# Four float32r products whose moving operand is read as two halves in turn

## The chip, the cores and the metric

The kernel runs on one core of a Trainium2 chip. The metric is the device time of one execution in microseconds (us). PE is TensorE's matmul side, PEld its weight loads, DVE is VectorE, ACT ScalarE, POOL GpSimd, SP the engine that issues most DMAs. In a product (matmul) the stationary operand is loaded into the array first; the moving operand is then streamed through it column by column, and the result goes to PSUM.

## The reference

```
X = fft(fft(x, axis=1), axis=2).real           # x: 8 x 3072 x 256
h = X @ w_in;  g = h - tanh(h);  y = g @ w_out # 256 -> 2048 -> 256, tokens: 8 * 3072
h = y @ w_in2                                  # 256 -> 1024
e = exp(h - max(h));  s = e / (sum(e) + 1e-9)
v = h * s                                      # then a layer norm over 1024, times g_ln
out = layernorm(v) * g_ln @ w_out2             # 1024 -> 256
```

All arrays are float32.

## The kernel before

The first stage (up to about 200 us) computes the transform along the sequence with cosine and sine tables in plain float32 (`products`, L445) and a few float32r corrections (`lone_products`, L457). The transform along the model dimension is folded into `w_in` (`fold_w_in`, L345). What is left of the transform goes to DRAM and comes back in 48 groups of 256 pairs of tokens (`load_z`), six groups for each of the 8 batches.

After that the kernel makes 768 steps: 48 groups `n` times 16 blocks `m` of 128 of the 2048 hidden features. A step holds, in the order in which each engine's instructions are issued:

- `ab` (L720): six float32r products with a moving operand of 256 columns of `zs`, into a tile `pab`. They make an even and an odd part.
- `act_out` of the step before: `g = h - t` on DVE (L754), then the split of `g` into `gh`: ACT rounds it to float32r (`rnd`, L152), and POOL makes the remainder (`rest`, L155).
- `act_in`: `asb`, and the sum and difference `h` on DVE (L727, L742, L743), then tanh on ACT (L749).
- `o1` of two steps before: six products (L773) with 512 columns of `gh` moving, summed over the 16 steps of a group in `x2p`.

The second layer is spread over the steps, one tile of 128 tokens in each four of them: `h2` (L806, twelve products with 512 columns of `wi2` moving, in two steps of six), `expo` and `soft` on DVE and ACT, a transpose by DVE and DMA, `split_moved` on ACT and POOL, and `outp` (L896, 24 products with 256 columns of `wo2` moving, in two steps of twelve). The order is written out by hand in the loop over the steps; no planner moves anything. Each engine works through its own queue in order.

Every float32r product is made as three passes: high part times high part, high times low, low times high. So each moving operand exists twice, as a rounded high part and a remainder, made by `rnd` and `rest`. `split_z` does so for `zs` in steps 9 and 11 of the group before it is used; `split_wi2` and `split_wo2` do it once for each half of the weights, in steps 10, 12, 18 and 19. The queue of SP carries the loads and stores; the change moves none of them.

The host puts the output's rows in order by a table (`out_rows`).

Of the kernel before, what the change touches and what calls it, by code (L numbers as in the profile page):

```python
# [19 lines left out]
B, S, D = 8, 3072, 256  # L20
FF1, FF2 = 2048, 1024
P = 128
# [5 lines left out]
GP = 256  # L28
GPB = PAIRS // GP
# [36 lines left out]
def columns():  # L66

    i = np.arange(NS)
    odd = 2 * i.reshape(NSJ, P) + 1
    return np.concatenate([np.stack([odd, S // 2 - odd], 1).reshape(-1), 4 * i + 2, 4 * i])  # L70
# [42 lines left out]
def out_rows():  # L113

    k = columns()
    plus = np.where(k % 4 == 3, k, (S - k) % S)
    minus = np.where(k % 4 == 3, S - k, k)
    minus[k == 0] = S // 2
    rows = np.stack([plus.reshape(GPB, GP), minus.reshape(GPB, GP)], 1).reshape(-1)
    return (np.arange(B)[:, None] * S + rows[None]).reshape(-1)  # L120


# [5 lines left out]
def fft2_moe_moe_kernel(  # L128
    ctx: ExitStack, tc: tile.TileContext, xr, x8, xn, xn8, w_in, w_out, w_in2, w_out2, g_ln, tt, t8, ft, out
):  # L130
    nc = tc.nc
# [19 lines left out]
    def rnd(o, i):  # L151
        nc.scalar.activation(out=o, in_=i, func=AF.Copy)  # L152

    def rest(eng, o, i, hi):
        eng.tensor_tensor(out=o, in0=i, in1=hi.bitcast(F32), op=ALU.subtract)  # L155

    def doubles(ap):

        return ap.bitcast(U32)
# [29 lines left out]
    wt = [wa.tile([P, 2, 2, 512], F32R, name=f"wt{c}") for c in range(4)]  # L189
# [35 lines left out]
    def split_z(n, u):  # L225
        zf, nb, zs = zg[n]
        if n % GPB >= NSJ:
            rnd(zs[:, 0, u], zf[:, u])
            rest(nc.gpsimd, zs[:, 1, u], zf[:, u], zs[:, 0, u])
        else:  # L230
            zc = zp.tile([P, GP], F32, tag="zc", bufs=1, name=f"zc{n}_{u}")
            for w, op in enumerate((ALU.add, ALU.subtract)):
                nc.gpsimd.tensor_tensor(out=zc[:, w * P : (w + 1) * P], in0=zf[:, u, :P], in1=zf[:, u, P:], op=op)
            rnd(zs[:, 0, u], zc)
            rest(nc.gpsimd, zs[:, 1, u], zc, zs[:, 0, u])


    coming, raws = [], {}
# [100 lines left out]
    def fold_w_in(c, w):  # L339

        pws = []
        for mt in range(2):
            pw = ps.tile([P, 512], F32, tag="ps", name=f"pw{c}_{mt}")
            for k in range(2):
                nc.tensor.matmul(  # L345
                    pw,
                    ftab[:, k, mt * P : (mt + 1) * P],
                    w[:, k * 512 : (k + 1) * 512],
                    start=(k == 0),
                    stop=(k == 1),  # L350
                )
            pws.append(pw)
        wf = fold.tile([P, 1024], F32, tag="cw", bufs=3, name=f"wf{c}").rearrange("p (m n) -> p m n", m=2)
        for mt, pw in enumerate(pws):
            rnd(wf[:, mt], pw)
        nc.gpsimd.dma_start(out=wnu_d[:, c * 512 : (c + 1) * 512], in_=wf[0:1, 1])
        rnd(wt[c][:, 0], wf)
        rest(nc.vector, wt[c][:, 1], wf, wt[c][:, 0])
        nc.gpsimd.memset(wt[c][0:1, :, 1].bitcast(F32), 0.0)
# [268 lines left out]
    def taken(banks, shape, tag, name):  # L628
        banks.append(banks.pop(0))
        return banks[-1].tile(shape, F32, tag=tag, name=name)  # L630


    wi2 = wp.tile([P, 2, 2, FF2], F32R, name="wi2")

    wi2_raw = [wk.tile([P, FF2], F32, tag="stage", name=f"wi2r_{k}") for k in range(2)]
# [1 line left out]
        nc.sync.dma_start(out=wi2_raw[k], in_=wi2_d[k])  # L637

    def split_wi2(k):
        rnd(wi2[:, 0, k], wi2_raw[k])  # L640
        rest(nc.gpsimd, wi2[:, 1, k], wi2_raw[k], wi2[:, 0, k])

    wo2 = wp.tile([P, 2, NK2, D], F32R, name="wo2")
    ident = wp.tile([P, P], F32, name="ident")
# [6 lines left out]
    wg = []  # L651
# [21 lines left out]
        )  # L673

    def split_wo2(half):
        g = wg[half][1]
        ks = slice(half * 4, half * 4 + 4)
        rnd(wo2[:, 0, ks], g)
        rest(nc.gpsimd, wo2[:, 1, ks], g, wo2[:, 0, ks])


    a1536 = wp.tile([P, NM, B], F32, name="a1536")
# [29 lines left out]
    x2p, x2s = {}, {}  # L712

    def ab(n, m):
        _, nb, zs = zg[n]
        c, o = m // 4, (m % 4) * P
        pab = p_ab.tile([P, 2, GP], F32, tag="ab", name=f"ab{n}_{m}")
        for u in range(2):
            for i, (hw, hz) in enumerate(PASSES):
                nc.tensor.matmul(  # L720
                    pab[:, u], wt[c][:, hw, u, o : o + P], zs[:, hz, u], start=(i == 0), stop=(i == 2)
                )
        return pab

# [40 lines left out]
    def o1(n, m):  # L765
        if m == 0:
            x2p[n] = [p_x2.tile([P, 2 * GP], F32, tag=f"x2_{mt}", name=f"x2p{n}_{mt}") for mt in range(2)]
        gh = gs.pop((n, m))
        c, k = divmod(m, 4)

        for i, (hw, hg) in enumerate(((0, 0), (1, 0), (0, 1))):
            for mt in range(2):
                nc.tensor.matmul(  # L773
                    x2p[n][mt],
                    wo1[c][:, hw, k, mt * P : (mt + 1) * P],
                    gh[:, hg],
                    start=(m == 0 and i == 0),
                    stop=(m == NM - 1 and i == 2),
                )
        if m == NM - 1:  # L780
            xs = wk.tile([P, 2, 2, 2 * GP], F32R, tag="x2s", name=f"x2s{n}")
            x2s[n] = xs
            if n == NG - 1:
                for mt, p in enumerate(x2p.pop(n)):
                    rnd(xs[:, 0, mt], p)
                    rest(nc.vector, xs[:, 1, mt], p, xs[:, 0, mt])
                return
            xf = wk.tile([P, 2, 2 * GP], F32, tag="stage", name=f"x2f{n}")
            for mt, p in enumerate(x2p.pop(n)):
                rnd(xf[:, mt], p)  # L790
            for mt in range(2):
                rnd(xs[:, 0, mt], xf[:, mt])
                rest(nc.gpsimd, xs[:, 1, mt], xf[:, mt], xs[:, 0, mt])
# [3 lines left out]
    def h2(n, i, f):  # L797
        xs = x2s[n]
        if f == 0:
            h2s[n, i] = taken(bank_h2, [P, FF2], "h2", f"ph2_{n}_{i}")  # L800
        ph = h2s[n, i]
        tk = slice(i * P, (i + 1) * P)
        fs = slice(f * 512, (f + 1) * 512)
        for k in range(2):
            for q, (hx, hw) in enumerate(PASSES):
                nc.tensor.matmul(  # L806
                    ph[:, fs],
                    xs[:, hx, k, tk],
                    wi2[:, hw, k, fs],
                    start=(k == 0 and q == 0),  # L810
                    stop=(k == 1 and q == 2),
                )
# [74 lines left out]
    def outp(n, i, half):  # L887
        if half == 0:
            pos[n, i] = taken(bank_o, [P, 512], "t", f"po{n}_{i}")
        po = pos[n, i]  # L890
        ut = uts.pop((n, i, half))
        for k4 in range(4):
            k = half * 4 + k4
            ks = slice(k4 * P, (k4 + 1) * P)
            for q, (hu, hw) in enumerate(PASSES):
                nc.tensor.matmul(  # L896
                    po[:, :D],
                    ut[:, hu, ks],
                    wo2[:, hw, k],
                    start=(k == 0 and q == 0),  # L900
                    stop=(k == NK2 - 1 and q == 2),
                )
        if half == 1:
            o = wk.tile([P, D], F32, tag="o", name=f"o{n}_{i}")
            nc.scalar.activation(out=o, in_=po[:, :D], func=AF.Copy, scale=sts.pop((n, i))[:, 10:11])  # L905
            r0 = (n * 4 + i) * P
            nc.sync.dma_start(out=out[r0 : r0 + P, :], in_=o)
            us.pop((n, i))
            pos.pop((n, i))
# [39 lines left out]
    for step in range(steps + 2):  # L949
        n, j = divmod(step, NM)  # L950
        if step < steps:
            pab = ab(n, j)
            asb = lead(n, j, pab) if n == 0 else None
# [9 lines left out]
        for s in (range(o1_done, min(s1 + 1, steps))):  # L963
            o1(*divmod(s, NM))
        o1_done = max(o1_done, min(s1 + 1, steps))
        layer2(step, False)
        if step in (4, 8):
            c = (4, 8).index(step) + 2
# [4 lines left out]
        if step in (10, 12):  # L973
            split_wi2((step - 10) // 2)
# [15 lines left out]
        if NM + 2 <= step < NM + 4:  # L990
            split_wo2(step - NM - 2)
        if j == 6 and 1 <= n and n + 1 < NG:
            load_z(n + 1)
        if 1 <= n and n + 1 < NG and j in (9, 11):
            split_z(n + 1, int(j > 9))
# [11 lines left out]
    for f in range(2):  # L1007
        outp(NG - 2, 1, f)
# [3 lines left out]
    for f in range(2):  # L1012
        outp(NG - 2, 2, f)
    for f in range(2):
        h2(*tiles[1], f)
# [64 lines left out]
```

## Time and profile before

| | |
|---|---|
| median of three timed runs | 2922.41 us (2921.7 to 2923.3) |
| the profiled execution: its span, from the first to the last instruction | 2923.9 us |
| granted TensorE clock over the span | 0.997 of full speed |
| instructions | 49792, of them 16799 products and as many weight loads |
| HBM read and written | 162.01 and 138.47 MB |

The page gives no other time of the profiled execution than its span, which lies 1.5 us above the median. A matmul's time in the trace runs from its start to its last result, so the times of products that follow each other overlap; what a product takes of the engine is seen in the distance from one start to the next. Busy time counts overlapping stretches once. An idle time belongs to the engine before which it stands, and behind `<-` is what ended it.

### The profile page before, as it was taken

The page shows a single profiled execution, that of the slowest core. Times are in us where ns is not written, and L with a number is a line of the kernel's source. Part 1 is how long each engine was busy: PE and PEld are TensorE (multiplying, and loading weights), DVE is VectorE, ACT ScalarE, POOL GpSimd, SP SyncE. Part 2 cuts the span into 40 slices and gives each one's busy share as a digit, 9 for nine tenths or more (in the row PEclk, how much of TensorE's full clock was granted, in tenths as well). Part 3 has the DMA queues.
Part 4 walks back from the last instruction along what each step waited for, and adds up shares of the span by engine and source line. Part 5 has one row for each costly group of instructions (what it writes and reads, how often), then busy time and mean ns, then how long its engine had stood idle before and what let it go on. Part 6 is the DMA issues. An engine that isn't in the chain of part 4 may idle for free. (4 is left out here: it accounts for less than half of the span.)

```text
span 2923.9 us, 49792 instructions
## 1 busy us (share of the span) xinstructions
PE 2881.3 (99%) x16799; PEld 2482.3 (85%) x16799; DVE 2403.0 (82%) x4818; ACT 1803.9 (62%) x3287; POOL 1965.2 (67%) x2413
## 2 busy tenths in 40 slices
PE   7899999999999999999999999999999999999999
PEld 3467888888888888888888888888888888888888
DVE  7897888888888888888888888888888888888885
ACT  2345666666666666666666666666666666666665
POOL 0156767777677776777777767777677766777763
PEclk9999999999999999999999999999999999999999
DMA  8781333343334334344334433443434443443331
GB/s 306 252 298 31 88 94 94 90 94 92 87 94 98 89 89 99 88 94 93 89 95 91 96 89 90 97 91 90 94 92 92 93 92 88 95 98 89 89 91 42
DMA packets 876512, 303.75 MB, mean 104 GB/s; under 512 B 788520, under 2 KB 837688, under 8 KB 872960
## 3 DMA queue, kind: packets, MB, share of 16 engines
q1 hardware_dynamic: 873536, 293.95, 40.9%
q10 hardware_dynamic: 2304, 6.29, 0.5%
q8 instruction: 132, 2.16, 0.3%
q14 instruction: 124, 1.02, 0.1%
q0 software_dynamic: 416, 0.33, 0.0%
HBM read 162.01 MB, written 138.47 MB: 103 GB/s over the span
## 5 line engine op out<-in xcount | busy, mean ns | idle before, releaser
L155 POOL TENSOR_TENSOR gh<-g,gh 128x512 fp32r<-128x512 f32 x768 | 993.2, 1297 | 469.3 <-ACT gh L152 469.3
L773 PE MATMUL x2p<-gh,wo 128*128 128x512 f32 x4608 | 1206.5, 397 | 3.6 <-POOL gh L155 2.3
L773 PEld LDWEIGHTS x2p<-gh,wo 128*128 128x128 f32 x4608 | 825.5, 189 | 166.3 <-POOL gh L155 10.7
L749 ACT ACTIVATE t<-h 128x512 f32<-128x512 f32 x768 | 459.5, 598 | 547.8 <-DVE h L743 446.3
L720 PEld LDWEIGHTS ab<-zs,wt 128*128 128x128 f32 x4608 | 649.0, 188 | 72.5 <-DVE h L743 2.7
L720 PE MATMUL ab<-zs,wt 128*128 128x256 f32 x4608 | 668.0, 280 | 2.1 <-DVE h L743 2.1
L754 DVE TENSOR_TENSOR g<-h,t 128x512 f32<-128x512 f32 x768 | 521.8, 679 | 172.0 <-ACT t L749 168.5
L152 ACT ACTIVATE gh<-g 128x512 fp32r<-128x512 f32 x768 | 480.9, 626 | 235.5 <-DVE g L754 223.1
L896 PE MATMUL po<-wo,ut 128*128 128x256 f32 x4608 | 597.8, 278 | 4.4 <-ACT ut L152 2.6
L806 PE MATMUL ph<-wi,x2s 128*128 128x512 f32 x2304 | 597.1, 394 | 0.0
L896 PEld LDWEIGHTS po<-wo,ut 128*128 128x128 f32 x4608 | 560.7, 188 | 10.1 <-POOL ut L155 5.0
L727 DVE SCALAR_TENSOR_TENSOR asb<-nb,wnu,ab 128x256 f32<-128x256 f32 x768 | 367.1, 478 | 221.1 <-PE ab L720 219.3
L806 PEld LDWEIGHTS ph<-wi,x2s 128*128 128x128 f32 x2304 | 420.0, 188 | 84.5
L155 POOL TENSOR_TENSOR ut<-um,ut 128x512 fp32r<-128x512 f32 x372 | 480.8, 1292 | 0.8 <-issue 0.8
L743 DVE TENSOR_TENSOR h<-asb,ab 128x256 f32<-128x256 f32 x768 | 328.8, 428 | 26.5
L742 DVE TENSOR_TENSOR h<-asb,ab 128x256 f32<-128x256 f32 x768 | 329.1, 429 | 26.2
L819 ACT ACTIVATE e<-ph,st 128x1024 f32<-128x1024 f32 x192 | 214.3, 1116 | 97.9 <-DVE st L817 82.1
L817 DVE TENSOR_REDUCE st<-ph 128x1 f32<-128x1024 f32 x192 | 233.6, 1216 | 3.5 <-PE ph L806 3.5
L825 DVE SCALAR_TENSOR_TENSOR u<-ph,e 128x1024 f32<-128x1024 f32 x192 | 233.6, 1217 | 0.0
L152 ACT ACTIVATE ut<-um 128x512 fp32r<-128x512 f32 x372 | 231.1, 621 | 0.0
L856 DVE STREAM_TRANSPOSE tb<-u 128x1024 f32<-128x1024 f32 x186 | 230.0, 1236 | 0.0
L836 ACT ACTIVATE e<-u,st 128x1024 f32<-128x1024 f32 x192 | 219.5, 1143 | 0.0
(101 smaller groups left out, 1531.2 us busy)
## 6 DMA issues: line engine op xcount, KB each, us to landing
mv_d<-tb SPq DMA_DIRECT2D x186, 512.0 KB, 2.6
um<-mv_d SPq DMA_DIRECT2D x744, 128.0 KB, 3.8
out<-o SPq DMA_DIRECT2D x192, 128.0 KB, 1.7
x<-xr SPq DMA_DIRECT2D x23, 1024.0 KB, 7.6
z_d<-zt SPq DMA_DIRECT2D x16, 384.0 KB, 7.4
z_d<-zt ACTq DMA_DIRECT2D x16, 384.0 KB, 6.6
wo<-w_out SPq DMA_DIRECT2D x24, 256.0 KB, 5.5
zf<-z_d SPq DMA_DIRECT2D x48, 128.0 KB, 3.3
```

Source lines behind the costliest of these rows:

```text
L152: nc.scalar.activation(out=o, in_=i, func=AF.Copy)
L155: eng.tensor_tensor(out=o, in0=i, in1=hi.bitcast(F32), op=ALU.subtract)
L720: nc.tensor.matmul(pab[:, u], wt[c][:, hw, u, o : o + P], zs[:, hz, u], start=(i == 0), stop=(i == 2))
L727: nc.vector.scalar_tensor_tensor(out=asb, in0=zg[n][1], scalar=wnu[:, m : m + 1], in1=pab[:, 0], op0=ALU.mult, op1=ALU.add)
L742: nc.vector.tensor_tensor(out=h[:, 0], in0=asb, in1=pab[:, 1], op=ALU.add)
L743: nc.vector.tensor_tensor(out=h[:, 1], in0=asb, in1=pab[:, 1], op=ALU.subtract)
L749: nc.scalar.activation(out=t, in_=h, func=AF.Tanh)
L754: nc.vector.tensor_tensor(out=g, in0=hs.pop((n, m)).rearrange("p u n -> p (u n)"), in1=ts_.pop((n, m)).rearrange("p u n -> p (u n)"), op=A ...
L773: nc.tensor.matmul(x2p[n][mt], wo1[c][:, hw, k, mt * P : (mt + 1) * P], gh[:, hg], start=(m == 0 and i == 0), stop=(m == NM - 1 and i == 2),)
L806: nc.tensor.matmul(ph[:, fs], xs[:, hx, k, tk], wi2[:, hw, k, fs], start=(k == 0 and q == 0), stop=(k == 1 and q == 2),)
L817: nc.vector.tensor_reduce(out=st[:, 0:1], in_=ph, axis=AX.X, op=ALU.max, negate=True)
L896: nc.tensor.matmul(po[:, :D], ut[:, hu, ks], wo2[:, hw, k], start=(k == 0 and q == 0), stop=(k == NK2 - 1 and q == 2),)
```

## The change

In four products (`ab`, `o1`, `h2`, `outp`) the moving operand's access pattern is changed: instead of columns 0, 1, 2, ... of a row of 512 or 256 columns, TensorE reads column 0 of the first half, column 0 of the second half, column 1 of the first, and so on (`in_turn`). The results go to neighbouring places of PSUM in the order in which they come (`in_pairs` only gives the output the same shape). So the result's columns stand in another order than the operand's.

For `zs`, `wi2` and `wo2` that is undone beforehand: the splits now put the even columns into the first half and the odd ones into the second, so that reading in turn restores the old order. For `gh` it is not undone: the tokens of a group then stand as sum, difference, sum, difference instead of all sums and then all differences, and the host's table `out_rows` is changed to match.

```diff
-    rows = np.stack([plus.reshape(GPB, GP), minus.reshape(GPB, GP)], 1).reshape(-1)
+    rows = np.stack([plus, minus], 1).reshape(-1)
...
+    def in_turn(ap):
+        return ap.rearrange("p (h n) -> p n h", h=2)
+
+    def in_pairs(ap):
+        return ap.rearrange("p (n h) -> p n h", h=2)
+
+    def split_halves(eng, hi, lo, whole):
+
+        by_half = whole.rearrange("p (n h) -> p h n", h=2)
+        hi, lo = (a.rearrange("p (h n) -> p h n", h=2) for a in (hi, lo))
+        rnd(hi, by_half)
+        rest(eng, lo, by_half, hi)
...
         if n % GPB >= NSJ:
-            rnd(zs[:, 0, u], zf[:, u])
-            rest(nc.gpsimd, zs[:, 1, u], zf[:, u], zs[:, 0, u])
+            split_halves(nc.gpsimd, zs[:, 0, u], zs[:, 1, u], zf[:, u])
...
     def split_wi2(k):
-        rnd(wi2[:, 0, k], wi2_raw[k])
-        rest(nc.gpsimd, wi2[:, 1, k], wi2_raw[k], wi2[:, 0, k])
+        raw = wi2_raw[k].rearrange("p (f n h) -> p f h n", f=2, h=2)
+        hi, lo = (wi2[:, q, k].rearrange("p (f h n) -> p f h n", f=2, h=2) for q in range(2))
+        rnd(hi, raw)
+        rest(nc.gpsimd, lo, raw, hi)
...
     def split_wo2(half):
-        g = wg[half][1]
+        g = wg[half][1].rearrange("p k (n h) -> p k h n", h=2)
         ks = slice(half * 4, half * 4 + 4)
-        rnd(wo2[:, 0, ks], g)
-        rest(nc.gpsimd, wo2[:, 1, ks], g, wo2[:, 0, ks])
+        hi, lo = (wo2[:, q, ks].rearrange("p k (h n) -> p k h n", h=2) for q in range(2))
+        rnd(hi, g)
+        rest(nc.gpsimd, lo, g, hi)
...
                 nc.tensor.matmul(
-                    pab[:, u], wt[c][:, hw, u, o : o + P], zs[:, hz, u], start=(i == 0), stop=(i == 2)
+                    in_pairs(pab[:, u]),
+                    wt[c][:, hw, u, o : o + P],
+                    in_turn(zs[:, hz, u]),
...
                 nc.tensor.matmul(
-                    x2p[n][mt],
+                    in_pairs(x2p[n][mt]),
                     wo1[c][:, hw, k, mt * P : (mt + 1) * P],
-                    gh[:, hg],
+                    in_turn(gh[:, hg]),
...
-                    ph[:, fs],
+                    in_pairs(ph[:, fs]),
                     xs[:, hx, k, tk],
-                    wi2[:, hw, k, fs],
+                    in_turn(wi2[:, hw, k, fs]),
...
-                    po[:, :D],
+                    in_pairs(po[:, :D]),
                     ut[:, hu, ks],
-                    wo2[:, hw, k],
+                    in_turn(wo2[:, hw, k]),
```

## Rows read from the trace of the kernel before

**Rows 1.** The page's busy line: busy us (share of the span) and count for each engine.

```profile
PE 2881.3 (99%) x16799; PEld 2482.3 (85%) x16799; DVE 2403.0 (82%) x4818; ACT 1803.9 (62%) x3287; POOL 1965.2 (67%) x2413
```

**Rows 2.** Windows, two stretches: us, busy us (count) by engine, granted clock, DMA share, GB/s.

```profile
700.00:1500.00 800.00, 799.90 (x4797) 705.49 (x4796) 665.30 (x1361) 515.79 (x941) 574.68 (x709) 1.00 0.40 93
2870.00:2924.00 54.00, 47.41 (x314) 42.02 (x312) 26.60 (x55) 26.99 (x51) 13.24 (x35) 1.00 0.07 22
```

**Rows 3.** The page's costliest groups: line, operation, tiles, shapes, count, busy us, mean ns, idle.

```profile
L773 PE MATMUL x2p<-gh,wo 128*128 128x512 f32 x4608 | 1206.5, 397 | 3.6 <-POOL gh L155 2.3
...
L720 PE MATMUL ab<-zs,wt 128*128 128x256 f32 x4608 | 668.0, 280 | 2.1 <-DVE h L743 2.1
...
L896 PE MATMUL po<-wo,ut 128*128 128x256 f32 x4608 | 597.8, 278 | 4.4 <-ACT ut L152 2.6
L806 PE MATMUL ph<-wi,x2s 128*128 128x512 f32 x2304 | 597.1, 394 | 0.0
```

**Rows 4.** Timeline of PE in two stretches: start us, us, engine, line, operation, count.

```profile
236.39 3.62 PE L666 MATMUL cm<-wg,ones 128*128 128x256 f32 x16
...
1500.28 0.87 PE L720 MATMUL ab<-zs,wt 128*128 128x256 f32 x6
1500.99 1.56 PE L773 MATMUL x2p<-gh,wo 128*128 128x512 f32 x6
1502.39 1.55 PE L806 MATMUL ph<-wi,x2s 128*128 128x512 f32 x6
1503.78 0.87 PE L720 MATMUL ab<-zs,wt 128*128 128x256 f32 x6
...
1507.98 1.54 PE L896 MATMUL po<-wo,ut 128*128 128x256 f32 x12
1509.36 1.56 PE L773 MATMUL x2p<-gh,wo 128*128 128x512 f32 x6
...
1514.26 0.87 PE L720 MATMUL ab<-zs,wt 128*128 128x256 f32 x6
```

**Rows 5.** Products by line: count, shortest/median/longest ns, first and last start, forms.

```profile
L457 PE MATMUL pz<-t8s,hl x48: 326/326/687, 30.8 to 191.2; 96*128 96x384 f32 x40, 96*128 96x388 f32 x8
...
L345 PE MATMUL pw<-wi_f,ftab x32: 592/593/1061, 66.6 to 144.3; 128*128 128x512 f32 x32
...
L666 PE MATMUL cm<-wg,ones x16: 378/379/379, 236.4 to 239.6; 128*128 128x256 f32 x16
```

**Rows 6.** L806 alone, from 700 to 1500 us and from 2870 us on.

```profile
L806 PE MATMUL ph<-wi,x2s x684: 390/393/404, 703.7 to 1491.7; 128*128 128x512 f32 x171
...
L806 PE MATMUL ph<-wi,x2s x60: 388/393/477, 2875.1 to 2907.1; 128*128 128x512 f32 x60
```

**Rows 7.** Timeline of PE: twelve products of 8 columns.

```profile
245.09 1.40 PE L697 MATMUL pa<-zh,wt 128*128 128x8 f32 x12
```

**Rows 8.** Waits of DVE, PE and the weight loads: us in total, times, longest us.

```profile
DVE asb L727 <- PE ab L720: 219.3, 475, 3.6
DVE g L754 <- ACT t L749: 168.5, 212, 1.7
...
PE x2p L773 <- POOL gh L155: 2.3, 6, 0.7
...
PEld x2p L773 <- POOL gh L155: 10.7, 26, 1.1
```

**Rows 9.** Groups by line and shape: splits of zs, and two reads by ACT.

```profile
L155 POOL TENSOR_TENSOR zs<-zc,zs 128x256 fp32r<-128x256 f32 x48 | 48.0, 1000 | 31.7 <-ACT zs L152 31.7
...
L155 POOL TENSOR_TENSOR zs<-zf,zs 128x256 fp32r<-128x256 f32 x48 | 35.6, 742 | 13.9 <-ACT zs L152 13.9
...
L152 ACT ACTIVATE zs<-zf 128x256 fp32r<-128x256 f32 x48 | 19.8, 413 | 0.0
...
L329 ACT ACTIVATE wo_f<-wo 128x1024 f32<-128x1024 f32 x6 | 6.9, 1155 | 8.5 <-DVE pm L405 4.3 <-DMA nb<-nu_d 2.4 <-ACT zt L494 1.7
...
L152 ACT ACTIVATE wt<-wf 128x1024 fp32r<-128x1024 f32 x4 | 4.2, 1057 | 0.1
```

More of the change, by code (lines that the diff above doesn't have):

```diff
@@ L233, in split_z @@
                 nc.gpsimd.tensor_tensor(out=zc[:, w * P : (w + 1) * P], in0=zf[:, u, :P], in1=zf[:, u, P:], op=op)
-            rnd(zs[:, 0, u], zc)
-            rest(nc.gpsimd, zs[:, 1, u], zc, zs[:, 0, u])
+            split_halves(nc.gpsimd, zs[:, 0, u], zs[:, 1, u], zc)
     coming, raws = [], {}
@@ L720, in ab @@
                 nc.tensor.matmul(
-                    pab[:, u], wt[c][:, hw, u, o : o + P], zs[:, hz, u], start=(i == 0), stop=(i == 2)
+                    in_pairs(pab[:, u]),
+                    wt[c][:, hw, u, o : o + P],
+                    in_turn(zs[:, hz, u]),
+                    start=(i == 0),
+                    stop=(i == 2),
                 )
```

## The prediction, made before the changed kernel ran

> **What bounds the kernel now.** I read the busy shares first. PE is busy for 2881.3 of 2923.9 us [rows 1], and between 700 and 1500 us for 799.90 of 800 [rows 2]; DVE stands at 83% there, POOL at 72%, ACT at 64%, the DMA engines at 40%. The granted clock is 1.00, the 2.4 GHz level. Everything but the first 200 us or so and the last 40 goes at PE's pace, so the question is what one product costs.
>
> The groups by line give four products [rows 3]: L773 (o1, 4608 of 512 columns, 397 ns each), L806 (h2, 2304 of 512, 394 ns), L720 (ab, 4608 of 256, 280 ns) and L896 (outp, 4608 of 256, 278 ns). These means are durations from issue to the last result and overlap. What one takes of PE's time shows in the timeline [rows 4] as start to start: o1 (1502.39 - 1500.99)/6 = 233 ns, h2 (1503.78 - 1502.39)/6 = 232, ab (1500.99 - 1500.28)/6 = 118, outp (1509.36 - 1507.98)/12 = 115.
>
> At 2.4 GHz a column per cycle is 213.3 ns for 512 columns and 106.7 for 256. All four take more, and three other products of this kernel say that they need not [rows 5]. L457 is float32r too, with 384 columns, but its moving operand is the same four columns again and again: 326 ns, which is 160 + 166. L345 is plain float32 at two cycles a column, with 512 new columns in a row: 593 = 426.7 + 166. L666, plain float32 with 256 columns: 379 = 213.3 + 166. So 166 ns is what lies around the streaming, and a product without friction lasts its cycles plus 166: 379.3 for 512 float32r columns, 272.7 for 256. Against this the four have an excess of 17.7, 14.7, 7.3 and 5.3 ns. Since L457 (full pace, no new columns) and L345 (new columns, half pace) have none, the excess belongs to new moving columns taken one per cycle. It is not other engines' traffic: h2 has a median of 393 with the DMA engines 40% busy and of 393 again in the last 54 us, where they are 7% busy [rows 6]. Its spread is narrow too (390 to 404), so it looks like something that the order of addresses settles.
>
> The whole excess is 4608 x 17.7 + 2304 x 14.7 + 4608 x 7.3 + 4608 x 5.3 = 81.6 + 33.9 + 33.6 + 24.4 = 173.5 us.
>
> **The change part by part.** (1) The four products read column n of the first half, then column n of the second. The counts of products, columns and weight loads stay, and the output is still written to neighbouring addresses. No row of before reads two places in turn. Lower bound: the excess goes, -173.5 us. Upper bound: two cycles a column, the pace of L345 and L666; (593 - 397) x 4608 + (593 - 394) x 2304 + (379 - 280) x 4608 + (379 - 278) x 4608 = 903 + 458 + 456 + 465 = +2283 us. Between them stands the row nearest in kind, L457: it is the one float32r product with a moving pattern of two levels, it comes back to addresses just read, and it has no excess. [...]
>
> (2) Not all of that can be had in the 256-column products, since each has its own weight load. Twelve products of 8 columns at L697, each with a 128-column weight load, take 1.40 us, the last some 0.17 of it [rows 7]: (1.40 - 0.17)/11 = 112 ns each, which must be the weight loads' own pace (bounds 106.7, the streaming itself, and 1.40/12 = 117). From start to start a product has some 2.7 ns beside its cycles: L666's 16 take 3.62 us, the last 0.379 of it, so (3.62 - 0.379)/15 = 216 = 213.3 + 2.7 [rows 4]. A frictionless float32r product of 256 columns would so come every 109.4 ns, and 2.6 ns of its excess stay behind the weight loads: 4608 x (7.3 - 2.6) = 21.7 and 4608 x (5.3 - 2.6) = 12.4. The gain is 81.6 + 33.9 + 21.7 + 12.4 = 150 us.
>
> (3) What is late next. The period of four steps is 1514.26 - 1500.28 = 13.98 us [rows 4]; 150 us over 192 such periods is 0.78 us each, leaving 13.2. DVE waits for ab for 219.3 us in all [rows 8], or 1.14 us a period, so on average 0.36 us of slack stays there. The g and h of one step hang on ACT's tanh (168.5 us of DVE waits), which no faster PE shortens. PE itself waits for gh on POOL 6 times for 2.3 us and its weight loads 26 times for 10.7 us now; with o1 two steps behind, two steps of 0.19 us less, it meets gh late more often. I estimate 100 such meetings of 0.15 us, 15 us given back; bounds 0 and 60 (a wait of 0.3 us in each of the 192 periods).
>
> (4) split_z, split_wi2 and split_wo2 now read every second word. ACT does that at L329 already: 1155 ns for 1024 against 1057 for a copy from neighbouring addresses at L152 [rows 9], +10%, or some 40 ns on a split of zs. No row shows POOL reading so; its two kinds of zs parts take 742 and 1000 ns in the mean [rows 9]. Bounds for POOL: nothing more, or twice as long, 48 x 0.742 + 48 x 1.0 = 84 us of POOL's time. POOL idles a third of the span and zs is made five steps or more before it is read, so I cost it at nothing; uncovered, it is gh behind it in POOL's queue that comes late, at most those 84 us. The splits of wi2 and wo2 are four of 2.4 us on POOL, in steps in which layer 2 has not begun; nothing. The rows of the output go to other addresses by the host's table alone.
>
> The sum: 2923.9 - 150 + 15 = 2789 us for the profiled execution; the three timed runs have a median 1.5 us lower (2922.4), so 2787.
>
> [...]
>
> **The rivals.** [...] Chance 0.18.
> (B) The order does not matter: the excess belongs to the number of new columns at this pace, which stays. 2924 us, within 0.2% (some 6 us, about what a measurement of this kernel can tell from no change). For it: 512 columns have 2 to 3 times the excess of 256. Chance 0.09.
> (C) Half of it: the two halves lie 512 or 1024 bytes apart and get in each other's way part of the time, as the spread of 390 to 404 ns for one and the same shape suggests that places matter. 2923.9 - 75 = 2849 us. Chance 0.17.
> (D) The excess goes, but the chain tanh, g, gh takes over and gives back its upper bound: 2923.9 - 150 + 60 = 2834 us. For it: DVE at 83% would stand at 88%. Against it: the 1.14 us that it waits for ab in each period. Chance 0.08.
> The forecast has 0.48, with its own range of 2770 to 2825 us.
>
> **How the numbers follow.** Faster: 0.48 + 0.17 + 0.08 = 0.73; same 0.09; slower 0.18. [...] Below, 2750 is the whole excess gone with no floor from the weight loads; above, 2930 takes in (B).
>
> **What would show it.** The mean duration of L773 and L806 at 380 to 382 ns, and of L720 and L896 near 273 to 276, with the 256-column products starting every 112 ns or so: step (1) and (2) right. [...] Waits of PE for gh or ut well over 15 us: step (3) too low. If the durations fall but the span does not, DVE's waits for ab will have vanished. The forecast is wrong if the durations stay or rise, whatever the rest does.

## The result, and the profile after

The changed kernel takes 2839.5 us (2837.4 to 2841.5) against 2922.9 for the kernel before on the same chip: a ratio of 0.971, 95% interval 0.970 to 0.973. It is faster by 83 us where 135 were forecast, inside the stated range of 2750 to 2930 and above the forecast's own range of 2770 to 2825. The profiled execution's span is 2837.7 us.

The page after: busy time, and the four products (line, operation, tiles, shapes, count, busy us, mean ns, idle before them and what ended it). Their lines have moved: L773 is L793, L720 is L736, L896 is L916, L806 is L826.

```profile
PE 2742.0 (97%) x16799; PEld 2442.4 (86%) x16799; DVE 2394.9 (84%) x4818; ACT 1806.2 (64%) x3287; POOL 1950.6 (69%) x2413
...
L793 PE MATMUL x2p<-gh,wo 128*128 128x512 f32 x4608 | 1141.6, 381 | 35.8 <-POOL gh L155 22.4
...
L736 PE MATMUL ab<-zs,wt 128*128 128x256 f32 x4608 | 638.8, 275 | 2.3 <-DVE h L763 2.3
...
L916 PE MATMUL po<-wo,ut 128*128 128x256 f32 x4608 | 588.5, 276 | 28.1 <-POOL ut L155 24.4
...
L826 PE MATMUL ph<-wi,x2s 128*128 128x512 f32 x2304 | 559.8, 379 | 0.0
```

Against [rows 3] the means fell from 397, 280, 278 and 394 ns to 381, 275, 276 and 379. The products of 512 columns stand where a product without friction was put, at 379.3. But the idle time before o1 and outp rose from 3.6 and 4.4 us to 35.8 and 28.1, most of it ended by POOL. PE's busy time fell by 2881.3 - 2742.0 = 139 us, its idle time rose by (2837.7 - 2742.0) - (2923.9 - 2881.3) = 53 us, and 139 - 53 is the 86 us between the spans.

The timeline of PE in an undisturbed stretch of the changed kernel, beside [rows 4]:

```profile
1499.89 0.83 PE L736 MATMUL ab<-zs,wt 128*128 128x256 f32 x6
1500.56 1.46 PE L793 MATMUL x2p<-gh,wo 128*128 128x512 f32 x6
1501.86 1.46 PE L826 MATMUL ph<-wi,x2s 128*128 128x512 f32 x6
1503.15 0.83 PE L736 MATMUL ab<-zs,wt 128*128 128x256 f32 x6
...
1507.08 1.50 PE L916 MATMUL po<-wo,ut 128*128 128x256 f32 x12
1508.42 1.46 PE L793 MATMUL x2p<-gh,wo 128*128 128x512 f32 x6
...
1513.02 0.83 PE L736 MATMUL ab<-zs,wt 128*128 128x256 f32 x6
```

From start to start o1 takes (1501.86 - 1500.56)/6 = 217 ns, h2 (1503.15 - 1501.86)/6 = 215, ab (1500.56 - 1499.89)/6 = 112, outp (1508.42 - 1507.08)/12 = 112. The period of four steps is 13.13 us, from 13.98.

The waits of PE, of its weight loads and of DVE after (us in all, times, longest), beside [rows 8]:

```profile
PE po L916 <- POOL ut L155: 24.4, 24, 1.4
PE x2p L793 <- POOL gh L155: 22.4, 57, 0.8
...
PEld x2p L793 <- POOL gh L155: 64.5, 76, 1.5
...
DVE g L774 <- ACT t L769: 183.6, 213, 2.4
DVE asb L747 <- PE ab L736: 120.9, 325, 3.2
```

DVE waits for ab 98 us less, so the faster PE did use up slack there; 120.9 us of it are left. PE's wait for gh grew from 2.3 to 22.4 us, that of the weight loads for gh from 10.7 to 64.5, and outp's wait for ut, 24.4 us, was 1.2 before.

I also summed all distances from one product's start to the next from the 17th step on. What they exceed 112 and 216 ns by, in distances that exceed them by no more than 25 ns (the excess), was 79.4 us in o1, 36.9 in h2, 25.3 in ab and 13.6 in outp before, and is 0.6, 0.1, -3.3 and -1.5 after: 159 us gone. Larger distances (waits) sum to 18 us before and 92 after: 74 given back. 159 - 74 = 85. Of the 92, 39 stand in the fourth of a group's 16 steps (o1 behind gh), 31 in the fifteenth (outp behind ut) and 11 in the twelfth (o1 behind gh).

Here is the fourth step of one group and the fifteenth, POOL's timeline and then PE's in each (start us, us, engine, line, operation, count):

```profile
1114.64 2.53 POOL L155 TENSOR_TENSOR x2s<-x2f,x2s 128x512 fp32r<-128x512 f32 x2
1117.12 2.53 POOL L155 TENSOR_TENSOR gh<-g,gh 128x512 fp32r<-128x512 f32 x2
...
1116.79 1.03 PE L793 MATMUL x2p<-gh,wo 128*128 128x512 f32 x4
1118.46 0.70 PE L793 MATMUL x2p<-gh,wo 128*128 128x512 f32 x2 [0.65 <-DVE st L849]
...
1151.64 0.19 POOL L864 TENSOR_TENSOR st<-st 128x1 f32<-128x1 f32 x1 [0.97 <-ACT e L856]
1151.92 0.19 POOL L865 TENSOR_SCALAR st<-st 128x1 f32<-128x1 f32 x1
1152.19 0.55 POOL L868 TENSOR_TENSOR st<-st,mhalf 128x1 f32<-128x1 f32 x1
1152.82 0.19 POOL L869 TENSOR_TENSOR st<-st 128x1 f32<-128x1 f32 x1
1153.01 1.27 POOL L155 TENSOR_TENSOR ut<-um,ut 128x512 fp32r<-128x512 f32 x1
...
1152.89 0.39 PE L916 MATMUL po<-wo,ut 128*128 128x256 f32 x2
1154.33 1.38 PE L916 MATMUL po<-wo,ut 128*128 128x256 f32 x10 [1.05 <-POOL ut L155]
```

In the fourth step two remainders of x2s occupy POOL from 1114.64 to 1117.12; two remainders of gh, which were due, run after them, and the last two products of o1 start at 1118.46 instead of 1117.65 (1116.79 and four products of 216 ns). The timeline puts that wait down to a DVE instruction that ended nearby; POOL's first gh ends just then, at about 1118.4 (the two take 2.53 us from 1117.12 on). In the fifteenth step outp stops after two products until 1154.33, when POOL has made ut; ahead of ut in its queue stand four small operations on st, the first of which waited 0.97 us for ACT's square.

That wait alone does not make ut late. By the same distances, all of the 11 us in the twelfth step and 29 of the 31 in the fifteenth stand in the 22 groups (of 47) during which POOL makes the next group's zs by way of a sum and a difference, zc (L247); the other groups take zs straight from zf. The first two lines are from the group shown above, where zc and a wait for ACT's rounding stand just ahead in POOL's queue; the last two are from a group without zc, where POOL waited 1.10 us for the same square and outp's twelve products came without a gap:

```profile
1146.99 0.88 POOL L247 TENSOR_TENSOR zc<-zf 128x128 f32<-128x128 f32 x2
1148.53 0.74 POOL L155 TENSOR_TENSOR zs<-zc,zs 128x256 fp32r<-128x256 f32 x1 [0.66 <-ACT zs L152]
...
1042.00 0.19 POOL L864 TENSOR_TENSOR st<-st 128x1 f32<-128x1 f32 x1 [1.10 <-ACT e L856]
...
1044.74 1.50 PE L916 MATMUL po<-wo,ut 128*128 128x256 f32 x12
```

The fourth step's waits stand in all 47 groups, with zc or without. No run takes zc out of POOL's queue, so its part is read from the places and not tested.

### The profile page after: what moved, and what is told of

Its sections match the earlier page's. It is cut to its first block, busy times and chain, and to the rows that moved or that the text cites. A ratio compares the mean times of both kernels' runs of the same rounds, so it can differ in the third digit from the quotient of the medians.

```text
span 2837.7 us, 50135 instructions
## 1 busy us (share of the span) xinstructions
PE 2742.0 (97%) x16799; PEld 2442.4 (86%) x16799; DVE 2394.9 (84%) x4818; ACT 1806.2 (64%) x3287; POOL 1950.6 (69%) x2413
## 5 line engine op out<-in xcount | busy, mean ns | idle before, releaser
L793 PE MATMUL x2p<-gh,wo 128*128 128x512 f32 x4608 | 1141.6, 381 | 35.8 <-POOL gh L155 22.4
L793 PEld LDWEIGHTS x2p<-gh,wo 128*128 128x128 f32 x4608 | 821.3, 190 | 156.0 <-POOL gh L155 64.5
L736 PEld LDWEIGHTS ab<-zs,wt 128*128 128x128 f32 x4608 | 632.9, 191 | 44.2 <-PE ab L736 2.8
L736 PE MATMUL ab<-zs,wt 128*128 128x256 f32 x4608 | 638.8, 275 | 2.3 <-DVE h L763 2.3
L916 PE MATMUL po<-wo,ut 128*128 128x256 f32 x4608 | 588.5, 276 | 28.1 <-POOL ut L155 24.4
L916 PEld LDWEIGHTS po<-wo,ut 128*128 128x128 f32 x4608 | 549.2, 192 | 37.1 <-POOL ut L155 31.6
L826 PE MATMUL ph<-wi,x2s 128*128 128x512 f32 x2304 | 559.8, 379 | 0.0
L747 DVE SCALAR_TENSOR_TENSOR asb<-nb,wnu,ab 128x256 f32<-128x256 f32 x768 | 365.9, 476 | 127.4 <-PE ab L736 120.9
L826 PEld LDWEIGHTS ph<-wi,x2s 128*128 128x128 f32 x2304 | 421.2, 189 | 51.5
```

The source lines that it names most:

```text
L736: nc.tensor.matmul(in_pairs(pab[:, u]), wt[c][:, hw, u, o : o + P], in_turn(zs[:, hz, u]), start=(i == 0), stop=(i == 2),)
L747: nc.vector.scalar_tensor_tensor(out=asb, in0=zg[n][1], scalar=wnu[:, m : m + 1], in1=pab[:, 0], op0=ALU.mult, op1=ALU.add)
L793: nc.tensor.matmul(in_pairs(x2p[n][mt]), wo1[c][:, hw, k, mt * P : (mt + 1) * P], in_turn(gh[:, hg]), start=(m == 0 and i == 0), stop=(m = ...
L826: nc.tensor.matmul(in_pairs(ph[:, fs]), xs[:, hx, k, tk], in_turn(wi2[:, hw, k, fs]), start=(k == 0 and q == 0), stop=(k == 1 and q == 2),)
L916: nc.tensor.matmul(in_pairs(po[:, :D]), ut[:, hu, ks], in_turn(wo2[:, hw, k]), start=(k == 0 and q == 0), stop=(k == NK2 - 1 and q == 2),)
```

## Experiments: what about the reading order helps

Three kernels change o1 alone, in the kernel before, and give each group of 256 pairs another reading order, by the group's number modulo 8. The output goes to neighbouring addresses in the order of reading; tokens come out permuted, and no value is left out. `read` gives the operand in the group's order, `laid` only gives the output the same shape. A piece is, in theory 2, four neighbouring columns, 16 bytes; below, two runs of four columns in turn take 379 ns and two runs of two 396.

```diff
                 nc.tensor.matmul(
-                    x2p[n][mt],
+                    laid(n, x2p[n][mt]),
                     wo1[c][:, hw, k, mt * P : (mt + 1) * P],
-                    gh[:, hg],
+                    read(n, gh[:, hg]),
```

> The kernel before, with o1 alone reading its 512 moving columns in another order in each group of 256 pairs, by the group's number modulo 8: 0 in a row; 1 two halves in turn; 2 four quarters in turn; 3 every second column, then the rest; 4 every fourth column, four rounds; 5 blocks of 8 columns, two runs of 4 in turn; 6 blocks of 32, two runs of 16 in turn; 7 four columns of one half, then four of the other. The tokens of a group come out in another order; no value is left out. Mean duration of L773's successor in each group (379.3 ns without any excess, 397 in a row today). [...] Theory 2, no two neighbours from one piece: it is enough that the next column lies in another piece of memory: 380 in groups 1, 2, 4, 5, 6, 397 in 0, 3 between. [...]

> As the run before with other orders, by the group's number modulo 8: 0 every eighth column, 1 every sixteenth, 2 eight eighths in turn, 3 blocks of 4 with two runs of 2 in turn, 4 blocks of 16 with two runs of 8, 5 blocks of 128 with two runs of 64, 6 two columns of one half, then two of the other, 7 sixteen of one, then sixteen of the other. Token order changes, no value is left out. [...] Theory 2, no two neighbours from one piece: 380 in 0, 1, 2, 4, 5, and 397 in 3. [...]

> As the two runs with patterns, o1 alone, by the group's number modulo 8: 0 in a row; 1 halves in turn, but every second column of each, then the rest; 2 halves in turn, every fourth column of each; 3 sixteen sixteenths in turn; 4 blocks of 16 columns, four runs of 4 in turn; 5 blocks of 8, four runs of 2 in turn; 6 eight columns of one half, then eight of the other; 7 halves in turn, every eighth column of each. Token order changes, no value is left out. [...] Groups 3 and 4: if four places are bad for their number, 4 is near the 441 of four quarters; if for their distance, near 380; 3 is 692 or more.

The medians of the products' durations in one group of each kind (96 products each):

| order of the 512 columns | median ns |
|---|---|
| in a row (the first kernel and the third) | 396 |
| two halves in turn | 379 |
| blocks of 128, 32, 16 or 8 columns, two runs of 64, 16, 8 or 4 in turn | 379 |
| blocks of 4, two runs of 2 in turn | 396 |
| two halves in turn, every second column of each, then the rest | 397 |
| 16, 8, 4, 2 columns of one half, then as many of the other | 403, 406, 413, 502 |
| four quarters in turn; blocks of 16, four runs of 4 | 438; 433 |
| blocks of 8, four runs of 2 in turn | 514 |
| every second, fourth, eighth, sixteenth column | 634, 639, 610, 612 |
| two halves in turn, every fourth or eighth column of each | 635, 642 |
| eight eighths, sixteen sixteenths in turn | 692, 610 |

The first kernel's rows for one group each: in a row, two halves in turn, four quarters, every second column, blocks of 8 with two runs of 4 (count, shortest/median/longest ns, first and last start us):

```profile
L799 PE MATMUL x2p<-gh,wo x96: 391/396/400, 682.1 to 735.7; 128*128 128x512 f32 x96
...
L799 PE MATMUL x2p<-gh,wo x96: 377/379/411, 738.0 to 790.1; 128*128 128x512 f32 x96
...
L799 PE MATMUL x2p<-gh,wo x96: 434/438/453, 792.4 to 850.1; 128*128 128x512 f32 x96
...
L799 PE MATMUL x2p<-gh,wo x96: 614/634/642, 852.5 to 927.1; 128*128 128x512 f32 x96
...
L799 PE MATMUL x2p<-gh,wo x96: 377/379/379, 1007.4 to 1060.2; 128*128 128x512 f32 x96
```

The second kernel's: two runs of 2, and two runs of 8 in turn:

```profile
L799 PE MATMUL x2p<-gh,wo x96: 391/396/400, 931.6 to 985.4; 128*128 128x512 f32 x96
...
L799 PE MATMUL x2p<-gh,wo x96: 377/379/413, 987.7 to 1040.5; 128*128 128x512 f32 x96
```

Two places in turn help from a distance of four columns, 16 bytes, up to half the row (379 ns at each), and do nothing at two columns, 8 bytes (396). A far place is worth no more than a near one. Theory 2 (it is enough that neighbours lie apart) falls with every second to sixteenth column, at 610 to 639 ns: 0.87 to 0.92 ns a column beside the 166 ns, where L345's two cycles a column are 0.83, and so above the 593 ns that step (1) took as its upper bound. Two places help, more do not: four and eight places in turn, at 438 and 692 ns, are slower than a row.

The third kernel has strides in two halves in turn, and four places near each other. Its rows: halves in turn with every second column, with every fourth, blocks of 8 with four runs of 2, blocks of 16 with four runs of 4:

```profile
L799 PE MATMUL x2p<-gh,wo x96: 391/397/400, 772.1 to 825.7; 128*128 128x512 f32 x96
...
L799 PE MATMUL x2p<-gh,wo x96: 614/635/653, 828.0 to 902.6; 128*128 128x512 f32 x96
...
L799 PE MATMUL x2p<-gh,wo x96: 500/514/517, 1039.7 to 1103.3; 128*128 128x512 f32 x96
...
L799 PE MATMUL x2p<-gh,wo x96: 428/433/435, 980.6 to 1037.3; 128*128 128x512 f32 x96
```

One count goes with many of these durations. Take every second column of a reading order, and count how many of those in succession lie in the same piece. They are four with two runs of four or more columns in turn (379 ns), two in a row, with two runs of 2 and with every second column of two halves (396, 396 and 397), and one with a stride of two or more in a row, or of four or more in two halves (610 to 642). So four cost 0 ns, two cost 17 or 18, one costs 231 to 263. The count does not go with the rest. By it 16, 8 and 4 columns of one half and then as many of the other should all cost what a row costs, and they cost 7 to 17 ns more (403, 406 and 413). Four quarters and blocks of 16 with four runs of 4 have one column in succession and take 438 and 433 ns; two and two columns and blocks of 8 with four runs of 2 have one as well and take 502 and 514. Eight eighths take 692, which is more than any stride, and sixteen sixteenths 610, less than the 692 or more that was expected. For four places, 433 against 438 says that their number matters and their distance does not. The count describes durations; what inside TensorE makes them no trace shows.

## Experiments: which part of the change does what

o1 alone in turn, in the kernel before:

```diff
-                    x2p[n][mt],
+                    in_pairs(x2p[n][mt]),
...
-                    gh[:, hg],
+                    in_turn(gh[:, hg]),
...
-    rows = np.stack([plus.reshape(GPB, GP), minus.reshape(GPB, GP)], 1).reshape(-1)
+    rows = np.stack([plus, minus], 1).reshape(-1)
```

> The kernel before with the change made to o1 alone, and the output rows to match; ab, h2 and outp read in a row and the splits are as before. Theory (the reading itself): o1's mean falls from 397 to 380.5 ns as in the whole change, the other three stay at 280, 394 and 278, the gain is 4608 x 17.9 = 82 us less what PE then waits for POOL: 15 to 35 us of new waits at the pace of 3.41 us a step, so 2855 to 2875 us. Rival (the gain needs all four, or comes from the new order of the tokens): o1 stays at 390 or more and the time above 2900.

2882.6 us, ratio 0.9857 (0.9841 to 0.9874), 41 us faster. Its page's rows for o1 and outp:

```profile
L779 PE MATMUL x2p<-gh,wo 128*128 128x512 f32 x4608 | 1134.1, 380 | 9.5 <-POOL gh L155 7.4
...
L902 PE MATMUL po<-wo,ut 128*128 128x256 f32 x4608 | 604.7, 280 | 17.1 <-POOL ut L155 14.1
```

o1 has 380 ns, as in the whole change; outp, untouched, already idles 17.1 us. By the distances, o1's excess is gone (79.4 to -1.4 us), the waits rose from 18 to 46, and the excess of the other three by 12. 81 - 28 - 12 = 41; the 12 us, which the expectation did not have and whose cause stays open, put the time 8 us above it.

Its complement, all but o1 (the inverse of the diff above, on the changed kernel):

> The changed kernel with o1 reading in a row again (its tokens and the output rows as before); ab, h2 and outp read in turn. Theory: their excess over 112 and 216 ns from start to start, some 80 us, goes, o1 keeps 397 ns, and at this pace PE's waits grow by 25 to 45 us: 2870 to 2890 us. Rival (products of 256 columns gain nothing, being held by their weight loads): only h2's 36 us go, 2890 to 2905 us, with ab and outp still at 118 and 116 ns from start to start.

2880.9 us, ratio 0.9848 (0.9834 to 0.9863), 44 us faster. Its four products:

```profile
L793 PE MATMUL x2p<-gh,wo 128*128 128x512 f32 x4608 | 1218.2, 398 | 9.8 <-POOL gh L155 5.6
...
L736 PE MATMUL ab<-zs,wt 128*128 128x256 f32 x4608 | 638.2, 275 | 2.3 <-DVE h L763 2.3
...
L916 PE MATMUL po<-wo,ut 128*128 128x256 f32 x4608 | 584.0, 276 | 21.2 <-POOL ut L155 17.2
...
L826 PE MATMUL ph<-wi,x2s 128*128 128x512 f32 x2304 | 560.1, 379 | 0.0
```

The products of 256 columns gain as well, so the rival falls. By the distances the excess of ab, h2 and outp is gone (-3.9, -0.1 and -1.5 us), o1 keeps 79, and the waits rose from 18 to 53. 41 + 44 = 85 against 83 for both: the times of the parts add up, each with waits of its own.

## Experiments: where the missing gain went

Two places in POOL's queue are moved in the changed kernel. The split of ut is issued ahead of the square, whose small operations on POOL wait for ACT; and the two remainders of x2s go one each into the next two steps, behind that step's gh.

```diff
-    x2p, x2s = {}, {}
+    x2p, x2s, x_rests = {}, {}, []
...
             for mt in range(2):
                 rnd(xs[:, 0, mt], xf[:, mt])
-                rest(nc.gpsimd, xs[:, 1, mt], xf[:, mt], xs[:, 0, mt])
+                x_rests.append((xs, xf, mt))
...
         at = tile_at(step, 8)
+        at12 = tile_at(step, 12)
+        if at12 and q < 2:
+            split_moved(*at12, q)
         if at and q == 0:
             square(*at)
             if 4 * at[0] + at[1] <= last_moved:
                 turn(*at)
-        at = tile_at(step, 12)
-        if at:
-            if q < 2:
-                split_moved(*at, q)
-            else:
-                outp(*at, q - 2)
+        if at12 and q >= 2:
+            outp(*at12, q - 2)
...
         out_done = max(out_done, min(step - lag + 1, steps))
+        if x_rests:
+            xs, xf, mt = x_rests.pop(0)
+            rest(nc.gpsimd, xs[:, 1, mt], xf[:, mt], xs[:, 0, mt])
```

> The changed kernel with two places moved in POOL's queue and none of the arithmetic: the split of ut is issued ahead of the square and its five small POOL operations in the step that holds both, and the two remainders of x2s go one into each of the next two steps, behind that step's gh, instead of both ahead of it. Theory (what the change gave back are PE's waits for gh and ut, which stand behind those operations in POOL's queue, 74 us in all): the waits fall to 5 to 20 us and the time to 2770 to 2785 us. Rival (the chain h, tanh, g on DVE and ACT is what is late, and POOL only its last link): the waits move to other steps, time 2820 to 2840 us.

2761.0 us (2759.2 to 2762.5), ratio to the kernel before 0.9440 (0.9426 to 0.9454): 163 us faster than before and 78 faster than the change alone, under the expected 2770. It beats both kernels. The window of 700 to 1500 us (as in [rows 2]), PE's wait for gh, and DVE's for ab:

```profile
700.00:1500.00 800.00, 800.00 (x5114) 738.86 (x5113) 699.44 (x1445) 549.27 (x1004) 610.43 (x763) 1.00 0.43 98
...
PE x2p L793 <- POOL gh L155: 3.3, 6, 0.8
...
DVE asb L747 <- PE ab L736: 65.4, 187, 3.5
```

PE is busy for 800.00 of 800 us again, from 782.65 in the changed kernel. Its large distances sum to 16 us, as before the change (18). The fall from 92 to 16 is 76 us, the whole gain; the expectation missed because it took the 74 us given back for all the waits there were. DVE's wait for ab went on falling, to 65 us: the chain on DVE and ACT was not what held PE, and the rival falls.

Each move by itself:

> The changed kernel with one of the two moves in POOL's queue alone: the split of ut ahead of the square and its small operations. Theory (POOL's queue, two separate places of lateness): the waits of outp for ut, 34 us in all, go; those of o1 in the fourth step of each group stay at about 40: 2800 to 2812 us. Rival (one common backlog): the fourth step's waits grow or shrink with it, and the time is under 2785 or above 2825 us.

> The changed kernel with the other move alone: the two remainders of x2s one step and two steps later, each behind that step's gh. Theory (two separate places): o1's waits in the fourth step of each group, 39 us in all, go, those of outp for ut stay: 2795 to 2810 us. Rival (one common backlog): under 2785 or above 2825 us.

With ut first 2792.8 us (0.9549, 0.9533 to 0.9565), with x2s later 2804.3 (0.9589, 0.9575 to 0.9603). Against 2839.5 that is 47 and 35, together 82; both at once gave 78. So these are two separate places, though not wholly: ut first also took 10 of the 11 us in the twelfth step and 8 of the 39 in the fourth, and beat its expectation by 7 us. PE's waits on POOL that are left, first with ut first, where 0.4 us are left for ut:

```profile
PE x2p L793 <- POOL gh L155: 15.5, 36, 0.8
```

and with x2s later:

```profile
PE po L916 <- POOL ut L155: 24.0, 24, 1.3
...
PE x2p L793 <- POOL gh L155: 7.0, 27, 0.8
```

Then both moves in the kernel before, which reads in a row:

> The kernel before, all products reading in a row, with both moves in POOL's queue. Theory (POOL was late only because PE became faster): PE's large waits, 18 us in all, fall to about 10, and the time to 2910 to 2923 us. Rival (the order alone is worth the 78 us that it gave the changed kernel): 2840 to 2860 us.

2917.4 us against 2925.2, ratio 0.9973 (0.9963 to 0.9984): 8 us, and PE's large waits fall from 18 to 10. The same two moves are worth 78 us with PE at 13.13 us a period and 8 us at 13.98. POOL's order cost the kernel before little; with the faster PE it cost about ten times as much.

## Why the prediction was right, and where a term was off

**What bounds the kernel** was right: PE's own pace, and in it an excess of products that read new float32r columns, 17.7 ns for one of o1. The cycles that the prediction counts at 2.4 GHz are in the traces as a pace: L345's 512 columns of plain float32 take 593 - 379 = 214 ns more than L666's 256 [rows 5], 0.84 ns a column at two cycles, and the changed h2 starts every 215 ns, 0.42 ns a column.

The time by itself would not tell this: 2839.5 us lies nearer to rival (C)'s 2849 and rival (D)'s 2834 than to the forecast's 2787. It is the products' means and distances that do.

**Step (1)** was right in its result. No row of before showed the whole excess of o1 and h2 going, 81.6 and 33.9 us in the sum; that was the author's estimate, and the runs showed 79.4 us falling to 0.6 and 36.9 to 0.1. Why the order of the columns matters no run shows. More places are not better: four take 438 ns and eight 692. L457 was the right row to lean on for a pattern of two levels at full pace, but it comes back to the same four columns and says nothing of a pattern that leaves them each time; every fourth column has two levels too and takes 639 ns.

**Step (2)** had 34 us for ab and outp down to 112 ns a product; 25.3 + 3.3 + 13.6 + 1.5 = 44 came. The sum took it from the excess in the durations, 4.7 and 2.7 ns a product; the starts in [rows 4], 118 and 115 ns, would have given 6 and 3, or 41 us. With o1 and h2 (79 and 37 against 81.6 and 33.9) the gain was 159 us where the sum had 150, and by luck those 9 us covered a part of what step (3) missed. That 112 is the pace of the weight loads was inferred from [rows 7]; no run took the weight loads away, so it is argued, not shown.

**Step (3)** is the term that was off: 15 us given back, bounds 0 and 60, and 74 measured. It counted DVE's slack as an average over a period, found 0.36 us left, and took PE's meetings with a late gh for small and scattered. They came at fixed places: 0.8 us in the fourth step of every group, where POOL's queue puts 2.5 us of x2s ahead of gh, and 1.3 us in the fifteenth step of about half the groups, where zc and the st operations that wait for ACT stand ahead of ut. DVE, on which the slack was counted, was not the engine that was late. The sign that the prediction had named for this came: PE's waits for gh and ut, 22.4 + 24.4 = 47 us, are well over 15. Rival (D) had the size (2834 us against 2838) but the wrong chain: it named tanh and g, and the runs show POOL's order.

**Step (4)** was right, or nearly, that the splits are hidden. Two rows after, beside [rows 9]:

```profile
L155 POOL TENSOR_TENSOR zs<-zf,zs 128x256 fp32r<-128x256 f32 x48 | 35.9, 748 | 13.7 <-ACT zs L152 13.7
...
L152 ACT ACTIVATE zs<-zf 128x256 fp32r<-128x256 f32 x48 | 23.4, 488 | 0.0
```

POOL takes the same with every second word (742 to 748 ns); ACT takes 18% more (413 to 488), not 10%. POOL waits for it, 50.2 us in all against 45.6 before, and PE waits for no zs. A little of that may be in the fifteenth step's waits. But with o1 alone changed and the splits as they were, 20 us of waits stand in that step already, all but 0.2 in the same 22 groups.

The slower kernel, at 0.18, did not come, but other orders are slower: every second to sixteenth column, one from each piece in succession by the count above, took 610 to 639 ns, 231 or more above the 379. **Rivals (B) and (C)** fall with the excess at zero. Measured in place of the sum: 2923.9 - 159 + 74 = 2839, against a span of 2837.7.

## What to carry to other kernels

Where one engine bounds a kernel, compare each of its instruction forms with its cycles plus the constant that frictionless forms of the same trace show, 166 ns here; where an excess is the same in every stretch, as that of h2 was (a median of 393 ns in both of [rows 6]), its operand's access pattern is a thing to try. Here that took h2 to 379 ns. After an engine has been made faster, look for its new waits by place in the loop, not by average slack: here the queue order of an engine at 69% gave back 74 of 159 us, and moving two issues fetched it again.

## What the runs showed of the hardware

- A float32r product that reads 512 new columns in a row takes 396 ns; with two places in turn, 16 to 1024 bytes apart, it takes 379, which is 166 ns and 0.42 ns a column.
- Every second to sixteenth column costs 610 to 639 ns, four places in turn 433 to 438 (514 in runs of two columns), eight 692. So a stride in the moving operand added 54 to 61% to the duration of a product of o1.
- Products of 8 columns, each with a 128-column weight load, come every 112 ns; with their excess gone the products of 256 columns also come every 112 ns, not every 109.4 as estimated for them without a floor.
